# Cluster-masked attention and a SwiGLU layer as one pass over head pairs: mask inside the K=128 score product, the feed-forward work of batch b-1 between the chunks of batch b, and the cast of v behind the last use of its buffer

## Chip, cores and metric

The kernel runs on one core of one Trainium2 chip. The metric is the device time of one execution in microseconds (us). Engines are named as the profile names them: PE is TensorE (matmul), PEld its weight loads, DVE is VectorE, ACT is ScalarE, POOL is GpSimd, and SP is SyncE, which here only issues DMAs.

## What is computed

The shapes are B=4 batches, H=8 heads, S=768 tokens, D=64, 16 clusters per head, d_model=512 and d_ff=1536. All inputs and the output are float32.

```
c_n      = centroids / (||centroids|| + 1e-6)               # per head, 16 x 64
q_assign = argmax over clusters of (q/||q||) . c_n          # the same for k
mask     = q_assign[:, :, :, None] == k_assign[:, :, None, :]
scores   = where(mask, q k^T / sqrt(D), -1e9)
attn     = softmax(scores)
x        = (attn v), heads side by side: 3072 tokens x 512
xn       = x / rms(x) * rms_g
out      = (silu(xn w_gate) * (xn w_val)) w_out             # 3072 x 512
```

## The kernel before

There are two stages, one after the other. The first loops over the 32 (batch, head) pairs. For each it loads q, k and v as six blocks of 128 tokens, and casts v to bf16 with a column of ones behind it (L69), which later gives the row sums. It transposes q and k on PE, one float32 block of 128x64 at a time (L93, L97), and two engines copy each result out of PSUM (a bf16 copy by ACT, a float32 copy by DVE). The cluster scores are float32 matmuls of 16 output partitions (L108, `scT_ps`); ACT copies them to SBUF, POOL takes the maximum over the 16 partitions (L113, `sc_max`), and DVE compares (L114). The result is a one-hot matrix of 16 x 768 for q and for k.

The attention matrix is made transposed, keys on partitions, in 12 tiles of 128x384. Each has two matmuls, the scores with 64 rows in use (L121, `sc_ps`) and the mask as the product of the two one-hot matrices with 16 rows in use (L123, `mk_ps`). ACT takes the exponential (L126) and DVE multiplies it by the mask into `pT` (L127). Then, for each of six groups of queries, six matmuls of 65 columns (L132, `acc`) give the weighted sum of v and the row sum, DVE divides (L134 to L136), and a DMA writes 128x64 to a buffer `x_scratch` in DRAM.

The second stage first loads the three weight matrices (3 MB each), casts them to bf16 on DVE (L154 to L161), and then takes 512 tokens at a time: it reads x back, normalizes, transposes on PE (L186), does the gate and value products (L194, L196, 512 columns each), SiLU on ACT (L199), the product on DVE (L200), the output product (L205), a copy and a store. ACT loads another function table whenever it goes from exp or SiLU to the square root and back.

Nothing is written out by hand as an order. The pools have two buffers for most tiles, and a scheduler orders the instructions of each engine.

## Time and profile before

| | before |
|---|---|
| time, median of 3 runs | 1065.87 us (1063.18 to 1066.9) |
| span of the profiled execution | 1065.2 us |
| PE, DVE, ACT, POOL busy | 908.9, 598.0, 508.9, 167.2 us |
| mean granted TensorE clock | 0.718 |

Only the profiled execution's span is recorded, not a separate time; the median of the runs is 0.7 us above that span. A busy PE is not a PE at its peak: the recorded length of a matmul has a tail that overlaps the next one, so the pace is read from one start to the next. Granted clock 1.00 is the upper of TensorE's two levels (2.4 GHz), 0.50 the lower (1.2 GHz).

### The profile page before, as it was taken

How to read it: one execution, taken by the hardware profiler on the slowest of the kernel's cores; microseconds unless marked ns; L12 is line 12 of the kernel's file. 1: busy time of each engine (PE TensorE's matmuls, PEld its weight loads, DVE VectorE, ACT ScalarE, POOL GpSimd, SP SyncE). 2: the span in 40 equal slices, each digit the busy share in tenths (PEclk: the TensorE clock that was granted, in tenths of full speed). 3: DMA queues.
4: the chain of work that ended last, by engine and by line, in shares of the span. 5: the costliest groups of instructions: out<-in, count | busy, mean ns of one | idle time of the engine just before them, and what ended most of it. 6: DMA issues, size and time to landing. Idle time of an engine off the chain costs nothing.

```text
span 1065.2 us, 11986 instructions
## 1 busy us (share of the span) xinstructions
PE 908.9 (85%) x3552; PEld 311.0 (29%) x3552; DVE 598.0 (56%) x1665; ACT 508.9 (48%) x1221; POOL 167.2 (16%) x72
## 2 busy tenths in 40 slices
...
DMA packets 114098, 41.82 MB, mean 39 GB/s; under 512 B 105328, under 2 KB 108400, under 8 KB 114032
## 3 DMA queue, kind: packets, MB, share of 16 engines
...
## 4 chain that ended last, share of the span: by engine, by line
PE 57%; issue 23%; POOL 7%; DVE 4%; ACT 4%; DMA 4%; POOLq 0%; SPq 0%; DVEq 0%; ACTq 0%
PE scT_ps L108 11%; PE mk_ps L123 9%; PE sc_ps L121 8%; POOL sc_max L113 6%; PE gps L194 6%; PE ops L205 6%; PE vps L196 6%; PE ttmp L97 4%; PE ttmp L93 3%; PE acc L132 3%; DMA wo_tmp<-in_moe_w_out_dram 1%; ACT scT_sb L111 1%; PE tps L186 1%; ACT xnT L187 1%; DMA wtmp<-in_moe_w_val_dram 1%
## 5 line engine op out<-in xcount | busy, mean ns | idle before, releaser
L127 DVE TENSOR_TENSOR pT<-p_e,mk_ps 128x384 bf16<-128x384 bf16 x384 | 209.9, 553 | 157.1 <-PE mk_ps L123 140.3
L113 POOL PARTITION_ALL_REDUCE sc_max<-scT_sb x64 | 166.1, 2602 | 598.7 <-ACT scT_sb L111 597.5
L123 PE MATMUL mk_ps<-q_ohT,k_ohT 16*128 16x384 bf16 x384 | 184.8, 498 | 45.5 <-DVE o_sb L136 41.1
L121 PE MATMUL sc_ps<-qT,kT 64*128 64x384 bf16 x384 | 182.8, 492 | 23.5 <-ACT p_e L126 22.0
L126 ACT ACTIVATE p_e<-sc_ps 128x384 bf16<-128x384 f32 x384 | 168.3, 483 | 18.0 <-DVE pT L127 11.7
L98 ACT CAST kT<-ttmp 64x128 bf16<-64x128 f32 x192 | 49.6, 258 | 175.9 <-PE ttmp L97 174.4
L111 ACT COPY scT_sb<-scT_ps 16x384 f32<-16x384 f32 x128 | 59.6, 466 | 107.9 <-PE scT_ps L108 107.8
L194 PE MATMUL gps<-xnT,wg 128*128 128x512 bf16 x288 | 106.3, 396 | 0.8 <-ACT sg L199 0.2
L196 PE MATMUL vps<-xnT,wv 128*128 128x512 bf16 x288 | 105.9, 394 | 0.0
L132 PE MATMUL acc<-v_bf,pT 128*128 128x65 bf16 x1152 | 93.9, 244 | 7.2 <-DVE o_sb L136 6.6
L123 PEld LDWEIGHTS <-k_ohT 16*128 16x128 bf16 x384 | 37.6, 100 | 212.7 <-issue 138.7
L132 PEld LDWEIGHTS <-pT 128*128 128x128 bf16 x1152 | 77.0, 131 | 57.5 <-DVE qT L95 22.1
L108 PE MATMUL scT_ps<-qT,c_nT 64*16 64x384 f32 x128 | 93.0, 829 | 0.1
L94 ACT CAST qT<-ttmp 64x128 bf16<-64x128 f32 x192 | 49.4, 257 | 86.1 <-PE ttmp L93 85.9
L97 PE MATMUL ttmp<-ident_f,k_in 128*64 128x128 f32 x192 | 79.7, 415 | 9.7 <-DVE kT L99 5.5
L108 PE MATMUL scT_ps<-kT,c_nT 64*16 64x384 f32 x128 | 87.0, 794 | 0.0
L200 DVE TENSOR_TENSOR gvT<-sg,vps 128x512 bf16<-128x512 f32 x72 | 47.7, 685 | 67.8 <-ACT sg L199 67.1
L93 PE MATMUL ttmp<-ident_f,q_in 128*64 128x128 f32 x192 | 79.9, 416 | 1.0 <-DVE qT L95 1.0
L187 ACT COPY xnT<-tps 128x128 bf16<-128x128 bf16 x96 | 21.5, 266 | 105.0 <-DVE wo L161 51.4
L121 PEld LDWEIGHTS <-kT 64*128 64x128 bf16 x384 | 35.9, 101 | 108.1 <-issue 104.8
L186 PE MATMUL tps<-ident,xn 128*128 128x128 bf16 x96 | 19.6, 238 | 55.2 <-ACT xnT L187 53.7
L205 PE MATMUL ops<-wo,gvT 128*128 128x512 bf16 x288 | 66.7, 379 | 0.0
...
## 6 DMA issues: line engine op xcount, KB each, us to landing
...
x_scratch<-o_sb SPq DMA_DIRECT2D x192, 16.0 KB, 1.5
...
wtmp<-in_moe_w_gate_dram SPq DMA_DIRECT2D x1, 3072.0 KB, 10.0
...
```

The source lines that it names most:

```text
L93: nc.tensor.transpose(ttmp, q_in[:, t, :], ident_f32)
L97: nc.tensor.transpose(ttmp2, k_in[:, t, :], ident_f32)
L108: nc.tensor.matmul(scT_ps, lhsT=c_nT, rhs=src_T[:, m * MM:(m + 1) * MM], start=True, stop=True)
L113: nc.gpsimd.partition_all_reduce(sc_max, scT_sb, NC, bass_isa.ReduceOp.max)
L121: nc.tensor.matmul(sc_ps, lhsT=kT[:, kc, :], rhs=qT_flat[:, m * MM:(m + 1) * MM], start=True, stop=True)
L123: nc.tensor.matmul(mk_ps, lhsT=k_ohT[:, kc * P:(kc + 1) * P], rhs=q_ohT[:, m * MM:(m + 1) * MM], start=True, stop=True)
L126: nc.scalar.activation(p_e, sc_ps, ACT.Exp, scale=scale)
L127: nc.vector.tensor_mul(pT[:, kc, m * MM:(m + 1) * MM], p_e, mk_ps)
L132: nc.tensor.matmul(acc, lhsT=pT[:, kc, qg * P:(qg + 1) * P], rhs=v_bf[:, kc, :], start=(kc == 0), stop=(kc == ST - 1))
L194: nc.tensor.matmul(gps, lhsT=wg[:, dc, fc * P:(fc + 1) * P], rhs=xnT[:, dc, :], start=(dc == 0), stop=(dc == DC - 1))
L196: nc.tensor.matmul(vps, lhsT=wv[:, dc, fc * P:(fc + 1) * P], rhs=xnT[:, dc, :], start=(dc == 0), stop=(dc == DC - 1))
L205: nc.tensor.matmul(ops, lhsT=gvT[:, fc, s * P:(s + 1) * P], rhs=wo[:, fc, :], start=(fc == 0), stop=(fc == FC - 1))
```

## The change

The program becomes one pass over 32 slots, one per (batch, head), in an order that is written out by hand (`tc.manual_schedule()`). A slot has 9 chunks, each a score tile of 128x512, so there are 288 chunks.

- **Mask in the score matmul.** The tiles `aug` hold, on 128 partitions, 64 rows of transposed q or k in bf16, 16 one-hot rows and zeros. On q's side the one-hot rows are 0 for the token's cluster and -2048 elsewhere, so one matmul over K=128 adds -2048 to each score whose clusters differ, and the exponential makes it zero. `mk_ps` and the DVE multiply are gone.
- **Head pairs.** Two heads are transposed together, as 128x128 float32 blocks, in groups of four (`t_group`), with one copy of 512 columns per group. POOL casts into `aug` (`casts`) and into `vbf` (`casts_v`). The cluster scores are four float32 matmuls of 32 output columns that lie at partitions 0, 32, 64 and 96 of one PSUM tile (`assign`). DVE transposes them, takes the maximum along the free axis and compares, and eight DMAs put the one-hot rows into `aug` (`argmax1`, `argmax2`).
- **x stays on chip.** One division per slot writes into `x_t`; there is no `x_scratch`.
- **Feed-forward between the chunks.** Chunk 87 is the first that carries a piece of the layer for batch 0; from there each chunk of batch b carries one piece for batch b-1, which is four matmuls of 384 columns (gate or value) or three of 512 (output). There are 288 such pieces, and 12 empty ones at the beginning. What is left when the chunks end, all of batch 3, follows as a tail. SiLU becomes `tanh` and a DVE operation, so that all of ACT's functions but the first square root are in one table.
- **Weights** are loaded and cast in 12 parts during the first slots.
- **Place of the v cast.** For pair pi, `casts_v` stands at step 9 of the pair before, which is behind the last use of that `vbf` buffer (steps 2 to 7 of the same slot, for the second head of pair pi-2).

The core of the diff (`+` lines are in program order, and everything of the old body is removed):

```diff
+MASK = 2048.0
...
-    x_scratch = nc.dram_tensor("x_scratch", (n_tokens, d_model), BF16, kind="Internal").ap()
...
-                        sc_ps = ps.tile([P, MM], F32, tag="scores")
-                        mk_ps = ps.tile([P, MM], F32, tag="mask")
-                        nc.tensor.matmul(sc_ps, lhsT=kT[:, kc, :], rhs=qT_flat[:, m * MM:(m + 1) * MM],
-                                         start=True, stop=True)
-                        nc.tensor.matmul(mk_ps, lhsT=k_ohT[:, kc * P:(kc + 1) * P], rhs=q_ohT[:, m * MM:(m + 1) * MM],
-                                         start=True, stop=True)
-                        p_e = sb1.tile([P, MM], BF16, tag="p_e")
-                        nc.scalar.activation(p_e, sc_ps, ACT.Exp, scale=scale)
-                        nc.vector.tensor_mul(pT[:, kc, m * MM:(m + 1) * MM], p_e, mk_ps)
...
+    ps_sc = ctx.enter_context(tc.tile_pool(name="ps_sc", bufs=2, space=PSUM))
+    ps_gv = ctx.enter_context(tc.tile_pool(name="ps_gv", bufs=2, space=PSUM))
+    ps_d = ctx.enter_context(tc.tile_pool(name="ps_d", bufs=1, space=PSUM))
+    ps_pv = ctx.enter_context(tc.tile_pool(name="ps_pv", bufs=1, space=PSUM))
+    ps_t = ctx.enter_context(tc.tile_pool(name="ps_t", bufs=2, space=PSUM))
...
+    def load_pair(pi):
+        b, hp = divmod(pi, NP)
+        tiles = []
+        for src, nm in ((q, "q_in"), (k, "k_in")):
+            tl = ld.tile([P, ST, 2, D], F32, name=nm, tag=nm)
+            for a in range(2):
+                nc.sync.dma_start(out=tl[:, :, a, :],
+                                  in_=src[b, 2 * hp + a].rearrange("(p t) d -> p t d", p=P))
+            tiles.append(tl)
+        tl = ld.tile([P, 2, ST * D], F32, name="v_in", tag="v_in")
+        nc.sync.dma_start(
+            out=tl, in_=v[b, 2 * hp:2 * hp + 2].rearrange("h (p t) d -> p h (t d)", p=P))
+        tiles.append(tl)
+        loads[pi] = tiles
...
+            tl = const.tile([P, 2, S], BF16, name=f"aug{i}{a}")
+            nc.gpsimd.memset(tl, 0.0)
+            row.append(tl)
+        aug.append(row)
+        tl = const.tile([P, 2, ST, D + 1], BF16, name=f"vbf{i}")
+        nc.gpsimd.memset(tl, 1.0)
+        vbf.append(tl)
+    D0 = (0, D)
+    O0 = (D, 0)
...
+    def w_load(i):
+        kind, j = divmod(i, 4)
+        wt = stage.tile([P, DF], F32, name="wt", tag="wt", bufs=4)
+        if kind < 2:
+            src = (moe_w_gate, moe_w_val)[kind]
+            nc.sync.dma_start(out=wt, in_=src[j * P:(j + 1) * P, :])
...
+        def t_group(g):
+            if g == 0:
+                qk32[0] = prep.tile([P, 2 * S], F32, name="qk32", tag="qk32")
+            q_in, k_in, v_in = loads[pi]
+            tp = ps_t.tile([P, 4, P], F32, name="tp", tag="t")
+            for i in range(4):
+                side, t = divmod(4 * g + i, ST)
+                src = (q_in, k_in)[side]
+                nc.tensor.transpose(tp[:, i, :], src[:, t, :, :].rearrange("p a d -> p (a d)"), ident_f)
+            dst = qk32[0][:, g * 512:(g + 1) * 512]
+            if g == 1:
+                nc.vector.tensor_copy(dst, tp[:, :, :].rearrange("p a b -> p (a b)"))
+            else:
+                nc.scalar.copy(dst, tp[:, :, :].rearrange("p a b -> p (a b)"))
+        def casts():
+            for a in range(2):
+                r = slice(D0[a], D0[a] + D)
+                nc.gpsimd.tensor_copy(aug[st][a][r, :, :].rearrange("p s n -> p (s n)"), qk32[0][r, :])
+        def casts_v():
+            v_in = loads[pi][2]
+            for a in range(2):
+                nc.gpsimd.tensor_copy(vbf[st][:, a, :, 0:D],
+                                      v_in[:, a, :].rearrange("p (t d) -> p t d", d=D))
...
+        def assign():
+            hp = pi % NP
+            sp = ps_t.tile([P, HS], F32, name="sp", tag="t")
+            for j in range(4):
+                nc.tensor.matmul(sp[32 * j:32 * j + 32, :], lhsT=cbd[:, hp, :],
+                                 rhs=qk32[0][:, j * HS:(j + 1) * HS], start=True, stop=True,
+                                 tile_position=(0, 32 * j))
+            state["sp"] = sp
+        def argmax1():
+            tr = prep.tile([P, HS], F32, name="tr", tag="tr")
+            nc.vector.transpose(tr, state["sp"])
+            mx = small.tile([P, HS // NC], F32, name="mx", tag="mx")
+            trv = tr[:, :].rearrange("p (n c) -> p n c", c=NC)
+            nc.vector.tensor_reduce(mx, trv, axis=AX, op=ALU.max)
+            state["tr"], state["mx"] = trv, mx
+        def argmax2():
+            oh = prep.tile([P, HS], BF16, name="oh", tag="oh")
+            nc.vector.tensor_tensor(oh[:, :].rearrange("p (n c) -> p n c", c=NC), state["tr"],
+                                    state["mx"].unsqueeze(2).to_broadcast([P, HS // NC, NC]), op=ALU.is_ge)
+            nc.vector.tensor_scalar(oh[0:64, :], oh[0:64, :], scalar1=1.0, scalar2=MASK,
+                                    op0=ALU.subtract, op1=ALU.mult)
+            ohT = prep.tile([P, HS], BF16, name="ohT", tag="ohT")
+            nc.vector.transpose(ohT, oh)
+            for a in range(2):
+                for j in range(4):
+                    side, half = divmod(j, 2)
+                    nc.sync.dma_start(
+                        out=aug[st][a][O0[a]:O0[a] + NC, side, half * HS:(half + 1) * HS],
+                        in_=ohT[32 * j + NC * a:32 * j + NC * a + NC, :])
+        return [lambda: t_group(0), lambda: t_group(1), lambda: t_group(2), casts, assign, argmax1, argmax2, casts_v]
...
+    def score_chunk(slot, j):
+        pi, a = divmod(slot, 2)
+        ag = aug[pi % 2][a]
+        if j == 0:
+            pts[slot] = ptp.tile([P, ST * S], BF16, name="pT", tag="pT")
+        sc = ps_sc.tile([P, CH], F32, name="sc", tag="sc")
+        lo = j * CH
+        while lo < (j + 1) * CH:
+            kc, qo = divmod(lo, S)
+            n = min((j + 1) * CH - lo, S - qo)
+            o = lo - j * CH
+            nc.tensor.matmul(sc[:, o:o + n], lhsT=ag[:, 1, kc * P:(kc + 1) * P],
+                             rhs=ag[:, 0, qo:qo + n], start=True, stop=True)
+            lo += n
+        nc.scalar.activation(pts[slot][:, j * CH:(j + 1) * CH], sc, ACT.Exp, scale=scale)
...
+    def pv_group(slot, g):
+        pi, a = divmod(slot, 2)
+        vb = vbf[pi % 2]
+        if g == 0:
+            accs[slot] = ps_pv.tile([P, ST, D + 1], F32, name="acc", tag="acc")
+        acc = accs[slot]
+        for kc in range(ST):
+            nc.tensor.matmul(acc[:, g, :], lhsT=pts[slot][:, kc * S + g * P:kc * S + (g + 1) * P],
+                             rhs=vb[:, a, kc, :], start=(kc == 0), stop=(kc == ST - 1))
+    def pv_norm(slot):
+        b, h = divmod(slot, H)
+        if h == 0:
+            x_t[b] = xp.tile([P, ST, DM], BF16, name="x", tag="x")
+        acc = accs.pop(slot)
+        inv = small.tile([P, ST, 1], F32, name="inv", tag="inv")
+        nc.vector.reciprocal(inv, acc[:, :, D:D + 1])
+        nc.vector.tensor_tensor(x_t[b][:, :, h * D:(h + 1) * D], acc[:, :, 0:D],
+                                inv.to_broadcast([P, ST, D]), op=ALU.mult)
...
+        def sumsq(t):
+            if t == 0:
+                st["ss"] = small.tile([P, ST], F32, name="ss", tag="ss")
+                st["jk"] = xp.tile([P, 2, DM], BF16, name="jk", tag="jk")
+            if t % 2 == 0:
+                nc.scalar.activation(st["jk"][:, 0, :], x_t[b][:, t, :], ACT.Square,
+                                     accum_out=st["ss"][:, t:t + 1])
+            else:
+                nc.vector.scalar_tensor_tensor(st["jk"][:, 1, :], x_t[b][:, t, :], 1.0, x_t[b][:, t, :],
+                                               op0=ALU.mult, op1=ALU.mult, accum_out=st["ss"][:, t:t + 1])
+        def inv():
+            ir = small.tile([P, ST], F32, name="ir", tag="ir")
+            nc.gpsimd.tensor_scalar(ir, st["ss"], scalar1=1.0 / DM, scalar2=eps, op0=ALU.mult, op1=ALU.add)
+            nc.gpsimd.tensor_tensor(ir, ir, mhalf, op=ALU.pow)
+            st["ir"] = ir
...
+    def ffn_piece(n, kind, tail):
+        half = n // FC
...
+            if kind == 0 and fc == 0:
+                gvT[half] = ffn.tile([P, FC, HS], BF16, name="gvT", tag="gvT")
+            w = (wg, wv)[kind]
+            pool, tag = (ps_sc, "sc") if tail and n % 2 else (ps_gv, "gv")
+            pt = pool.tile([P, CH], F32, name=("gp", "vp")[kind], tag=tag)
+            for dc in range(DC):
+                nc.tensor.matmul(pt[:, :HS], lhsT=w[:, dc, fc * P:(fc + 1) * P],
+                                 rhs=xnT[b][:, dc, m * HS:(m + 1) * HS],
+                                 start=(dc == 0), stop=(dc == DC - 1))
+            if kind == 0:
+                th = ffn.tile([P, HS], F32, name="th", tag="th")
+                nc.scalar.activation(th, pt[:, :HS], ACT.Tanh, scale=0.5)
+                uu = ffn.tile([P, HS], F32, name="uu", tag="uu")
+                def after():
+                    nc.vector.scalar_tensor_tensor(uu, th, 1.0, pt[:, :HS], op0=ALU.add, op1=ALU.mult)
+                cur[n] = uu
+            else:
+                uu = cur.pop(n)
+                def after():
+                    nc.vector.tensor_tensor(gvT[half][:, fc, :], uu, pt[:, :HS], op=ALU.mult)
+            pend.append(after)
+        elif kind == 2 and half >= 1:
+            hf = half - 1
+            b, m = divmod(hf, 2)
+            t = m * TH + fc // 4
+            qd = fc % 4
+            if qd == 0:
+                pool, tag = (ps_pv, "acc") if tail and (fc // 4) % 2 else (ps_d, "d")
+                cur["d"] = pool.tile([P, DM], F32, name="dp", tag=tag)
+            dp = cur["d"]
+            for i in range(3):
+                f = qd * 3 + i
+                tl = fc // 4
+                nc.tensor.matmul(dp, lhsT=gvT[hf][:, f, tl * P:(tl + 1) * P], rhs=wo[:, f, :],
...
+    def at(slot, step, fn):
+        slot += step // NCH
+        extra.setdefault((slot, step % NCH), []).append(fn)
+    for pi in range(1, B * NP):
+        s0 = 2 * (pi - 1)
+        parts = prep_parts(pi)
+        for fn, step in zip(parts, (1, 3, 5, 6, 8, 9, 10, 9)):
+            at(s0, step, fn)
+        if pi + 1 < B * NP:
+            at(s0, 8, lambda pi=pi: load_pair(pi + 1))
+    for i in range(4):
+        at(0, i, lambda i=i: w_load(i))
+    for i in range(12):
+        at(2, 3 * i, lambda i=i: w_cast(i))
+        if i + 4 < 12:
+            at(2, 3 * i + 1, lambda i=i: w_load(i + 4))
+    for b in range(B):
+        steps = (8, 8, 9, 9, 10, 10, 11, 11, 12, 12, 13, 13)
+        for fn, step in zip(rms_parts(b), steps):
+            at(H * (b + 1), step, fn)
+    FFN0 = 15
+    for slot in range(NS):
+        for j in range(NCH):
+            score_chunk(slot, j)
+            done = slot * NCH + j
+            limit = min(B, max(0, (done - FFN0) // (H * NCH))) * 2 * FC
+            ffn_next(limit)
+            flush(1)
+            if slot > 0 and 2 <= j < 2 + ST:
+                pv_group(slot - 1, j - 2)
+            if slot > 0 and j == 2 + ST:
+                pv_norm(slot - 1)
+            for fn in extra.get((slot, j), ()):
+                fn()
...
+    for j in range(2 * NCH):
+        slot = NS
+        ffn_next(2 * FC * (B - 1) + (FC if False else 0), tail=False)
+        flush(1)
+        if 0 <= j < ST:
+            pv_group(NS - 1, j)
+        if j == ST:
+            pv_norm(NS - 1)
+        for fn in extra.get((NS + j // NCH, j % NCH), ()):
+            fn()
+    while ffn_next(NU + FC, tail=True):
+        flush(1)
+    flush()
```

The order on PE changes throughout. Before, inside a head of the first stage, this is what stands there; `sc_ps` and `mk_ps` alternate, and the transposes of the next head (`ttmp`) stand between:

```order
L121 MATMUL sc_ps<-qT,kT 128x384
L123 LDWEIGHTS k_ohT
L123 MATMUL mk_ps<-q_ohT,k_ohT 128x384
L97 MATMUL ttmp_383<-ident_f_63,k_in 64x128
L121 LDWEIGHTS kT
L121 MATMUL sc_ps<-qT,kT 128x384
```

After, in a chunk of a slot past chunk 87, one group of four transposes of the next pair ends the chunk before, then come one score matmul of 512 columns and the first matmuls of a gate piece; six `acc` matmuls follow behind the fourth `gp`:

```order
L184 MATMUL tp<-ident_f,k_in 128x128 x4
L253 LDWEIGHTS aug_127
L253 MATMUL sc<-aug_127 128x512
L339 LDWEIGHTS wg
L339 MATMUL gp<-xnT,wg 128x384
```

The mask matmul has left, and feed-forward matmuls stand behind every score tile. On SP, which issues every DMA, this is the beginning of the first stage before:

```order
L64 DMA q_in<-in_q_dram 128x6x64
L65 DMA k_in<-in_k_dram 128x6x64
L66 DMA v_in<-in_v_dram 128x6x64
L72 DMA c_in<-in_centroids_dram 16x64
```

And this is SP after, from the first weight loads to the one-hot rows of the third pair:

```order
L152 DMA wt<-in_moe_w_gate_dram 128x1536 x4
L76 DMA q_in<-in_q_dram 128x6x64 x2
L76 DMA k_in<-in_k_dram 128x6x64 x2
L80 DMA v_in<-in_v_dram 128x2x384
L232 DMA aug_133<-ohT 16x384 x4
L232 DMA aug_135<-ohT 16x384 x4
L152 DMA wt<-in_moe_w_val_dram 128x1536 x3
```

The eight DMAs that a pair's scores need stand behind the five loads of the pair after next, and in the first slots behind weight loads too.

## Rows read from the trace of the kernel before

**Rows 1.** The page's first part: busy time, share of span, instructions by engine.

```profile
PE 908.9 (85%) x3552; PEld 311.0 (29%) x3552; DVE 598.0 (56%) x1665; ACT 508.9 (48%) x1221; POOL 167.2 (16%) x72
```

**Rows 2.** Busy time by stretch: length, engines, granted clock (PEclk), DMA share, GB/s.

```profile
0.00:25.50 25.50, 11.60 (x26) 2.96 (x26) 10.16 (x41) 9.29 (x27) 6.11 (x10) 1.00 0.38 78
25.50:790.00 764.50, 680.73 (x2566) 213.00 (x2566) 474.34 (x1418) 380.69 (x965) 161.10 (x62) 0.65 0.13 28
790.00:836.50 46.50, 0.37 (x2) 0.24 (x3) 11.22 (x10) 0.28 (x2) 0.00 (x0) 0.50 0.55 204
836.50:1065.20 228.70, 216.22 (x958) 94.77 (x957) 102.27 (x198) 118.66 (x228) 0.00 (x0) 0.95 0.11 40
```

**Rows 3.** Groups of instructions by line: busy us, mean ns, idle before, releaser.

```profile
L113 POOL PARTITION_ALL_REDUCE sc_max<-scT_sb x64 | 166.1, 2602 | 598.7 <-ACT scT_sb L111 597.5 <-DVE q_ohT L114 1.1
L123 PE MATMUL mk_ps<-q_ohT,k_ohT 16*128 16x384 bf16 x384 | 184.8, 498 | 45.5 <-DVE o_sb L136 41.1 <-DVE k_ohT L114 3.5 <-DVE pT L127 0.9
L200 DVE TENSOR_TENSOR gvT<-sg,vps 128x512 bf16<-128x512 f32 x72 | 47.7, 685 | 67.8 <-ACT sg L199 67.1 <-PE vps L196 0.7
```

**Rows 4.** PE's instructions in order, first stage: start us, length us, what, count.

```profile
524.45 1.46 PE L108 MATMUL scT_ps<-qT,c_nT 64*16 64x384 f32 x2
525.84 0.49 PE L123 MATMUL mk_ps<-q_ohT,k_ohT 16*128 16x384 bf16 x1
526.26 0.42 PE L93 MATMUL ttmp<-ident_f,q_in 128*64 128x128 f32 x1
526.48 0.54 PE L132 MATMUL acc<-v_bf,pT 128*128 128x65 bf16 x6
526.82 0.41 PE L97 MATMUL ttmp<-ident_f,k_in 128*64 128x128 f32 x1
...
529.89 0.81 PE L108 MATMUL scT_ps<-kT,c_nT 64*16 64x384 f32 x2
530.63 0.20 PE L83 MATMUL cnt_ps<-ident_f,c_n 16*64 16x16 f32 x1
...
531.09 0.30 PE L97 MATMUL ttmp<-ident_f,k_in 128*64 128x128 f32 x1
531.32 0.82 PE L108 MATMUL scT_ps<-kT,c_nT 64*16 64x384 f32 x2
532.44 0.56 PE L132 MATMUL acc<-v_bf,pT 128*128 128x65 bf16 x12 [0.30 <-DVE o_sb L136]
532.93 0.49 PE L121 MATMUL sc_ps<-qT,kT 64*128 64x384 bf16 x2
```

**Rows 5.** Busy time in two short stretches, columns as in group 2.

```profile
529.00:535.00 6.00, 4.64 (x25) 1.42 (x23) 4.10 (x9) 5.22 (x11) 4.32 (x2) 0.93 0.37 78
...
876.00:880.00 4.00, 3.13 (x15) 1.48 (x14) 1.91 (x4) 2.62 (x12) 0.00 (x0) 0.75 0.40 131
```

**Rows 6.** PE's instructions in order, beginning of the second stage.

```profile
842.87 0.63 PE L196 MATMUL vps<-xnT,wv 128*128 128x512 bf16 x1
843.29 0.63 PE L194 MATMUL gps<-xnT,wg 128*128 128x512 bf16 x1
...
844.01 0.38 PE L194 MATMUL gps<-xnT,wg 128*128 128x512 bf16 x1
...
845.52 0.38 PE L196 MATMUL vps<-xnT,wv 128*128 128x512 bf16 x1
```

**Rows 7.** ACT's instructions in order: two exponentials, and two SiLU, back to back.

```profile
102.58 0.86 ACT L126 ACTIVATE p_e<-sc_ps 128x384 bf16<-128x384 f32 x2
...
849.14 1.08 ACT L199 ACTIVATE sg<-gps 128x512 f32<-128x512 f32 x2
```

**Rows 8.** POOL's memset of the identity, by line.

```profile
masks.py:197 POOL MEMSET ident_f<- 128x128 f32 x1 | 0.2, 204 | 0.0
```

**Rows 9.** DMA issues: KB each, median us from issue to landing.

```profile
x_scratch<-o_sb SPq DMA_DIRECT2D x192, 16.0 KB, 1.5
```

**Rows 10.** The last instruction on DVE, in order of time.

```profile
1061.63 0.69 DVE L207 COPY out_sb<-ops 128x512 f32<-128x512 f32 x1 [1.90 <-PE ops L205]
```

290 lines of the change are left out of this document (142 added, 148 removed).

## Prediction

> **What bounds the kernel now.** I read the busy time by stretch first, since the shares of the whole span mix stages. It shows three stages and a start [rows 2]: 25.5 us until the first full tile, 764.5 us of attention with PE busy 89% of it (680.7), 46.5 us in which PE does almost nothing while the weights arrive and are cast, and 228.7 us of feed-forward with PE busy 95%. So PE ends last in both long stages; DVE, the next, is busy 62% of the attention stretch (474.3 of 764.5), and 56% of the whole span [rows 1].
>
> Why attention takes PE so long is seen in its instructions in order [rows 4]. The reader should look at starts, not lengths. From the mask matmul at 525.84 to the transpose at 526.26 is 0.42 us. Its 384 columns need less: in the second stage a matmul of 512 columns takes the same 0.42 us from start to start as long as the clock is at its lower level (842.87 to 843.29), and 0.216 us afterwards (844.01 to 845.52 are seven intervals) [rows 6]. So 384 columns are worth 0.32 us at the lower level, and 0.10 us is the weight load, which lies bare where matmuls of 64 and 16 rows alternate. The second cause is the clock. The mean length of all 384 mask matmuls is 498 ns [rows 3], which is what single ones have at granted 0.50 (0.49 at 525.84), so nearly the whole stage runs at the lower level. It can rise: from about 529.9 on the same stage runs at the upper one, after a run of transposes, `acc` and float32 matmuls with no bare loads between [rows 4, 5]. A float32 matmul of 384 columns (two records) then takes 0.74 us from start to start (529.89 to 530.63) where it took 1.39 (524.45 to 525.84).
>
> **The change, in prices of these rows.** Taken away are 384 mask matmuls with about 0.42 us of pace each, their bare loads, the 46.5 us without PE work (the weights come in the first slots), `x_scratch` and its waits, and 64 all-reduces of 2602 ns on POOL [rows 3]. No PE work of the feed-forward is saved: 288 pieces of 1536 columns are the same columns as before. It cannot hide under attention either, if PE is the bound of both; what the interleaving does is fill PE. So I sum PE, and then ask whether another engine exceeds it.
>
> Prices at the upper level, and the lower in brackets:
> - bf16 columns with K=128: 512 in 0.216 (0.427) us [rows 6]. A slot's 4608 score columns cost 1.94 (3.84) us; a piece, 0.65 (1.28).
> - `acc`, 65 columns: twelve in 0.49 us (532.44 to 532.93), 0.041 each; six in 0.34 us at the lower level, 0.057 [rows 4]. 36 per slot: 1.48 (2.05) us.
> - float32 transpose: 0.23 (531.09 to 531.32) and 0.22 at the lower level when an `acc` follows (526.26 to 526.48) [rows 4]. No row has a stationary block of 128 float32 columns; here it was 64. From below, the clock could halve 0.22 to 0.11; from above, the load could double with its columns, which adds the 0.12 us by which 0.23 exceeds that, so 0.35. I take 0.23, the row nearest. 12 per pair, 6 per slot: 1.38 us (0.7 to 2.1; lower level 1.3).
> - `assign`: four float32 matmuls of 384 columns per pair. One after the other, 4 x 0.74 = 2.96 us (5.56) per pair, 1.48 (2.78) per slot [rows 4]. From below: all four at once, 0.37 per slot. I take one after the other, as every pair of such matmuls in the trace goes.
> - the transposes of x, 96 of 128 bf16 columns in all: under 0.3 us per slot by columns and a fixed part.
>
> A slot without feed-forward costs PE 1.94 + 1.48 + 1.38 + 1.48 = 6.3 us (10.0 at the lower level). A slot with nine pieces costs 9 x 0.65 + 6.3 + 0.3 = 12.4 us (22.0).
>
> The other engines, per slot. **ACT**: two SiLU of 512 columns back to back take 1.08 us, two exponentials of 384 take 0.86 [rows 7], so 0.54 and 0.43 each at most. Nine exponentials and one copy are 5.4 us, three tanh 1.3, squares and x copies about 0.4: 5.4 without and 7.1 us with feed-forward. **DVE**: no operation that it gets is wider than 512 columns but the weight casts and two copies of 768 per batch, and the 512-wide product out of PSUM takes 685 ns [rows 3]. Six feed-forward operations, two for the division, half of five for the one-hot rows, and about two for copies and norms: 12.5 x 0.685 = 8.6 us at most. **POOL** casts 2 x 1536 and 2 x 384 columns per pair, which no row shows. The memset, 128 columns in 204 ns [rows 8], gives 1.6 ns per column and 6.1 us per pair; the all-reduce, 768 in 2602 ns [rows 3], gives 3.4 and 13.0 us. I take the lower half, the memset being the simple streaming operation, but either fits under a pair's 12.6 us without feed-forward (nearly) and 24.8 with. So PE stays the bound of every slot, at either level of the clock, and the DVE and ACT work is covered by it. Should PE come out faster than these rows, DVE at up to 8.6 us would be next.
>
> **The sum.** Start: the chain to the first scores is the same kind as before (loads, transposes, cluster scores, maximum, one-hot rows), with DMAs in place of the all-reduce: 25 us, as now [rows 2]. Chunks 0 to 86 are 9.67 slots without feed-forward: 61 us at the upper level, 97 at the lower. I take 7.0 us per slot, 68, one fifth of the way: everything here has K=128, as in the stretch after which the clock rose [rows 4, 5], and no waits are due, but the first pairs share SP and the DMA engines with 9 MB of weights. Chunks 87 to 287 are 22.33 slots, 277 us less 12 empty pieces (7.8): 269. Then the last head: 15 pieces (9.8), `acc` 1.5, and a stand of about 3 us while the last x is normalized, since DVE and ACT must pass over it before PE can transpose. The tail is 72 + 12 = 84 pieces, 54.6 us. After the last matmul come a copy and a store, 3.6 us as now (1061.63 to the end of the span at 1065.2) [rows 10]. That is 72.5. Together 25 + 68 + 269 + 72.5 = 434.5, say 435 us against a span of 1065.2; the median of the runs lies 0.7 us above that span, which changes nothing here.
>
> **Where v's cast stands.** `casts_v` at step 9 comes after the last `acc` that reads its buffer (steps 2 to 7), so POOL does not stop there with the next pair's `casts` behind it. Its next reader is `acc` at step 2 of the second slot after, 11 or more chunks later, 8 us at 0.7 us per chunk: covered. Any earlier place would have made POOL wait up to that step, which the same margin covers at 1.4 us per chunk; I cost this part at nothing.
>
> **A rule against the serial price.** In the rows the cluster-score matmuls follow one another at 0.74 us, but they all write partitions 0 to 15 [rows 4]. The Trainium skill ("TensorE: Matmul & The Clock Gate", Part 3) says that matmuls whose outputs lie in different 32-partition strips run at the same time. No run here shows that so far. By it `assign` would be one matmul's time, not four.
>
> **Rivals.**
> - *The four cluster matmuls run together.* As a mechanism of this kernel: the pair pays 0.74 us, not 2.96; 1.1 us per slot over 32 slots is 35 us, and the time is 400. For it speaks that the four share the moving data's layout and write four strips; against it only that no row has it. With transposes at their low end as well, 378.
> - *The next pair is late.* The first scores of a pair need POOL's two casts and four of the eight DMAs, which stand on SP behind five loads, and land 1.5 us after issue if like `x_scratch` [rows 9]. The steps from 8 or 10 to 18 leave 5.6 to 7 us at 0.7 us per chunk, 11 or more with feed-forward. If PE stands 3 us at each of 15 pairs, the clock falls as well: with PE busy 3.13 of 4 us in the second stage the mean was 0.75 [rows 5], and 4 us at the lower level lose 2. That is 15 x 5 = 75 us, 510. For it: the chain crosses four engines. Against: the margin with feed-forward is double.
> - *The clock stays low.* If the small `acc` matmuls and the transposes keep it down as they mostly did: 25 + 97 + (22.33 x 22.0 - 12 x 1.28 = 476) + (15 + 84) x 1.28 + 2 + 5 + 3.6 = 735 us. Against: dense matmuls of K=128 had raised it by 844.0, 7.5 us into the second stage [rows 2, 6], and more than half of every slot's PE time is such.
> - *Slower than before: POOL's casts.* They gate every pair. The change loses from the point at which a pair takes 633 us / 15 = 42 us longer than 25, that is 67 us of POOL work, 17 ns per column. The dearest row has 3.4. Then 1068 us or more.
>
> **How the numbers follow.** The forecast, PE-bound at the upper level with cluster matmuls in sequence, 435 us, has 0.45; cluster matmuls together 0.28; pairs late 0.18; clock low 0.08; slower 0.01. The range from 378 (the second case with transposes at their low end) to 540 (pairs late, with transposes at their high end, 22 us, and a little more) leaves out the low clock and thin ends, about 0.15. A difference of 0.3% is about what a measurement of this kernel can tell from none; all cases but one are far beyond it: faster 0.98, same 0.01, slower 0.01.
>
> **What would show it.** In the changed profile PE should be busy nearly all of each slot from chunk 87 on, at granted clock near 1.00, with 11 to 12.5 us per slot, and 6 to 7 before; ACT and DVE well under PE; two table loads only; DMA landings and POOL's casts never on the chain of waits past the start. Whether the four `assign` matmuls start together or 0.74 us apart decides between the first two cases. The forecast is wrong if the granted clock is below 0.8 in the middle, if PE's idle time at a pair's first `sc` is put down to `aug`, or if ACT takes more per chunk than PE.

## The result, and the profile after

The changed kernel takes 419.35 us (median of 4 runs, 417.93 to 422.39) against 1064.53 us before, a ratio of 0.3946 with a 95% interval of 0.3929 to 0.3962. The forecast was 435 us, the range 378 to 540. The profiled execution has a span of 417.7 us and a mean granted clock of 0.939. Ratios, here and below, leave out any execution that is more than 1.5% above the fastest of its kernel.

The page's first part, and the beginning of its fourth (the chain that ended last), as answers to [rows 1]:

```profile
PE 355.3 (85%) x2972; PEld 219.9 (53%) x3009; DVE 224.8 (54%) x446; ACT 242.4 (58%) x460; POOL 80.5 (19%) x87
...
PE 75%; DVE 9%; SPq 4%; DMA 4%; ACT 3%; POOL 2%; issue 2%; POOLq 0%; DVEq 0%; ACTq 0%
```

PE is still what ends last, busy for the same 85% of a span that is 0.39 of the old one. This is the busy time by stretch of the changed kernel, cut at the first score matmul (20.2), the first gate piece (108.5), the end of the last chunk (341) and the first piece of the tail (358); columns as in [rows 2]:

```profile
0.00:20.20 20.20, 4.60 (x21) 2.76 (x22) 10.25 (x17) 3.94 (x5) 11.90 (x19) 0.89 0.55 120
20.20:108.50 88.30, 58.28 (x552) 38.33 (x554) 40.35 (x72) 54.55 (x104) 24.55 (x22) 0.81 0.62 183
108.50:341.00 232.50, 222.94 (x1994) 140.68 (x2021) 135.38 (x281) 161.33 (x306) 42.51 (x44) 0.98 0.25 65
341.00:358.00 17.00, 14.76 (x114) 8.94 (x115) 11.44 (x29) 5.72 (x14) 1.52 (x2) 0.90 0.05 16
358.00:417.70 59.70, 54.68 (x295) 29.24 (x299) 27.38 (x50) 16.84 (x34) 0.00 (x0) 1.00 0.12 45
```

The long stretch is as forecast: PE busy 96% of it, granted clock 0.98. The 88 us before it are not: PE is busy only 66%, the clock is at 0.81 in the mean, and the DMA engines are busy 62%. Against the terms of the sum:

| stretch | forecast, us | measured, us |
|---|---|---|
| start | 25 | 20.2 |
| chunks 0 to 86 | 68 | 88.3 |
| chunks 87 to 287 | 269 | 232.5 |
| last head and last x | 14.3 | 17.0 |
| tail with the last store | 58.2 | 59.7 |
| together | 434.5 | 417.7 |

Two large errors of opposite sign stand in this table, one of 20 and one of 36 us. PE's instructions in order, in the middle of the long stretch, show the second:

```profile
200.65 0.35 PE L267 MATMUL acc<-vbf,pT 128*128 128x65 bf16 x6
200.84 0.63 PE L184 MATMUL tp<-ident_f,k_in 128*128 128x128 f32 x4
201.31 0.38 PE L253 MATMUL sc<-aug 128*128 128x512 bf16 x1
201.53 0.81 PE L339 MATMUL gp<-xnT,wg 128*128 128x384 bf16 x4
202.18 0.35 PE L267 MATMUL acc<-vbf,pT 128*128 128x65 bf16 x6
...
204.38 0.85 PE L208 MATMUL sp<-qk,cbd 128*32 128x384 f32 x8
205.17 0.39 PE L253 MATMUL sc<-aug 128*128 128x512 bf16 x1
```

From start to start, a score tile of 512 columns takes 0.22 us and a gate piece 0.65, as priced. Six `acc` matmuls take 0.19 us (0.032 each, priced 0.041), four float32 transposes 0.47 (0.12 each, priced 0.23), and the four cluster matmuls 0.79 us together (204.38 to 205.17, eight records, priced 2.96). A slot is then 1.94 + 1.15 + 0.70 + 0.40 = 4.2 us without and 10.4 us with feed-forward, and 22.33 x 10.4 less 7.8 is 224 us. PE's idle time in the stretch is about the rest, 9.6 us (232.5 - 222.9); two thirds of it come when the transposes of x wait for DVE's norm (6.5 us in two places).

The first error is seen in who waited for whom, PE alone over the whole span (us in total, times, longest):

```profile
PE sc L253 <- DMA aug<-ohT: 26.1, 5, 6.9
PE xtp L313 <- DVE xn L306: 12.5, 4, 4.3
PE c_ps L135 <- DVE c L133: 8.7, 1, 8.7
PE sc L253 <- ACT pT L256: 4.7, 11, 0.5
PE acc L267 <- POOL vbf L199: 1.6, 1, 1.6
```

and in PE's order of time, where the scores of pairs 1, 2, 3 and 4 begin:

```profile
38.68 1.01 PE L253 MATMUL sc<-aug 128*128 128x512 bf16 x3 [6.29 <-DMA aug<-ohT]
...
57.12 1.01 PE L253 MATMUL sc<-aug 128*128 128x512 bf16 x3 [5.80 <-DMA aug<-ohT]
...
76.31 1.01 PE L253 MATMUL sc<-aug 128*128 128x512 bf16 x3 [5.61 <-DMA aug<-ohT]
...
90.40 0.59 PE L253 MATMUL sc<-aug 128*128 128x512 bf16 x3 [1.48 <-DMA aug<-ohT]
```

This is the rival of the late pair, but only in the pairs ahead of the feed-forward: 19.2 us of waits (the fifth, 6.9 us, belongs to the start), and behind the three long ones PE runs at the lower clock for a while (three score records take 1.01 us at 76.31 and 0.59 at 90.40). In the same stretch the first transposes of x wait 4.3 us for the norm, and one `acc` group 1.6 us for POOL's cast of v. Past chunk 87 there is no wait for one-hot rows. And since PE needs 4.2 us per slot ahead of the feed-forward and ACT, by the prediction's prices, 5.4, ACT and not PE would set the pace there if nothing were late: 9.67 x 5.4 = 52 us.

### The profile page after: what moved, and what is told of

Its sections match the earlier page's. It is cut to its first block, busy times and chain, and to the rows that moved or that the text cites. A ratio compares the mean times of both kernels' runs of the same rounds, so it can differ in the third digit from the quotient of the medians.

```text
span 417.7 us, 7771 instructions
## 1 busy us (share of the span) xinstructions
PE 355.3 (85%) x2972; PEld 219.9 (53%) x3009; DVE 224.8 (54%) x446; ACT 242.4 (58%) x460; POOL 80.5 (19%) x87
## 3 DMA queue, kind: packets, MB, share of 16 engines
HBM read 28.35 MB, written 6.29 MB: 83 GB/s over the span
## 4 chain that ended last, share of the span: by engine, by line
PE 75%; DVE 9%; SPq 4%; DMA 4%; ACT 3%; POOL 2%; issue 2%; POOLq 0%; DVEq 0%; ACTq 0%
PE vp L339 15%; PE sc L253 14%; PE gp L339 14%; PE dp L368 14%; PE acc L267 7%; PE tp L184 6%; DMA aug<-ohT 3%; PE xtp L313 3%; PE sp L208 2%; SPq L76 2%; DVE jk L294 2%; SPq L232 1%; ACT pT L256 1%; DVE oh L223 1%; DVE c L133 1%
## 5 line engine op out<-in xcount | busy, mean ns | idle before, releaser
L256 ACT ACTIVATE pT<-sc 128x512 bf16<-128x512 f32 x288 | 166.9, 598 | 77.8 <-PE sc L253 75.2
L253 PE MATMUL sc<-aug 128*128 128x256 bf16 (+1 forms) x381 | 111.4, 342 | 30.9 <-DMA aug<-ohT 26.1
L348 DVE SCALAR_TENSOR_TENSOR uu<-th,gp 128x384 f32<-128x384 f32 x96 | 53.0, 552 | 78.0 <-ACT th L344 78.0
L194 POOL CAST aug<-qk 64x1536 bf16<-64x1536 f32 x32 | 47.5, 1486 | 224.6 <-ACT qk L189 173.2
L339 PE MATMUL vp<-xnT,wv 128*128 128x384 bf16 x384 | 80.1, 332 | 1.7 <-DVE gvT L354 1.6
L339 PE MATMUL gp<-xnT,wg 128*128 128x384 bf16 x384 | 78.0, 326 | 0.0
L368 PE MATMUL dp<-wo,gvT 128*128 128x512 bf16 x254 | 69.1, 379 | 2.9 <-ACT ob L374 1.1
L267 PE MATMUL acc<-vbf,pT 128*128 128x65 bf16 x1152 | 69.6, 196 | 1.9 <-POOL vbf L199 1.6
L344 ACT ACTIVATE th<-gp 128x384 f32<-128x384 f32 x96 | 47.3, 492 | 40.9 <-PE gp L339 38.4
L354 DVE TENSOR_TENSOR gvT<-uu,vp 128x384 bf16<-128x384 f32 x96 | 52.6, 548 | 7.9 <-PE vp L339 1.3
```

The costliest lines, as they stand in the source:

```text
L194: nc.gpsimd.tensor_copy(aug[st][a][r, :, :].rearrange("p s n -> p (s n)"), qk32[0][r, :])
L253: nc.tensor.matmul(sc[:, o:o + n], lhsT=ag[:, 1, kc * P:(kc + 1) * P], rhs=ag[:, 0, qo:qo + n], start=True, stop=True)
L256: nc.scalar.activation(pts[slot][:, j * CH:(j + 1) * CH], sc, ACT.Exp, scale=scale)
L267: nc.tensor.matmul(acc[:, g, :], lhsT=pts[slot][:, kc * S + g * P:kc * S + (g + 1) * P], rhs=vb[:, a, kc, :], start=(kc == 0), stop=(kc == ...
L339: nc.tensor.matmul(pt[:, :HS], lhsT=w[:, dc, fc * P:(fc + 1) * P], rhs=xnT[b][:, dc, m * HS:(m + 1) * HS], start=(dc == 0), stop=(dc == DC ...
L344: nc.scalar.activation(th, pt[:, :HS], ACT.Tanh, scale=0.5)
```

## The experiments

**More cluster matmuls in one strip.**

```diff
-            for j in range(4):
+            for j in (0, 0, 0, 0, 1, 2, 3):
                 nc.tensor.matmul(sp[32 * j:32 * j + 32, :], lhsT=cbd[:, hp, :],
```

> The changed kernel with three more cluster matmuls per pair, all into the same 32 partitions as the first one (their result is overwritten with the same values). Theory: matmuls into one strip follow one another at 0.74 us, and only those into different strips share their time (the four of the changed kernel take 0.79 us together). Then 16 pairs x 3 x 0.74 = 36 us more, less what falls into waits in the first five pairs: 445 to 456 us. Rival: the short time of the four has nothing to do with strips (fewer passes for a block of 32 columns, say): then three more cost three times a quarter of 0.79, 0.6 us per pair, 10 us in all, 427 to 430.

Measured: 441.92 us (440.16 to 443.88), ratio 0.4145 (0.4128 to 0.4163), 22.6 us more than the changed kernel. PE's order in this run:

```profile
218.47 2.77 PE L208 MATMUL sp<-qk,cbd 128*32 128x384 f32 x14
221.16 0.39 PE L253 MATMUL sc<-aug 128*128 128x512 bf16 x1
```

Seven matmuls take 2.69 us, four times 0.67, where four in different strips took 0.79. So matmuls into one strip go one after the other, and those into other strips share their time. The profile is 24.4 us longer than the changed kernel's (442.1 against 417.7). Of these, 17.2 lie behind the first gate piece, where ten pairs with 1.90 us more each should give 19.0, and 7.2 ahead of it (it starts at 115.7, and not at 108.5), where six pairs give less because they wait anyway (their waits for one-hot rows fall from 26.1 to 23.2 us). The expectation had 0.74 us for each added matmul, and 0.63 (1.90 / 3) is what it cost; over 16 pairs that is 5 us, which covers the 3 us by which its window was missed.

**Feed-forward not interleaved.**

```diff
-            xnT[b] = xp.tile([P, DC, S], BF16, name="xnT", tag="xnT")
+            xnT[b] = xp.tile([P, DC, S], BF16, name="xnT", tag="xnT", bufs=4)
...
-            limit = min(B, max(0, (done - FFN0) // (H * NCH))) * 2 * FC
-            ffn_next(limit)
+            ffn_next(0)
...
-        ffn_next(2 * FC * (B - 1) + (FC if False else 0), tail=False)
+        ffn_next(0, tail=False)
```

> The feed-forward is not interleaved: all 288 pieces come after the last head (four buffers for the transposed x in place of two). Theory: interleaving hides the attention's ACT time and the pairs' hand-off under feed-forward matmuls. Chunks 87 to 287 then cost ACT's 5.4 us per slot or a little more instead of PE's 4.2, 22.33 x 5.4 to 6.5 = 121 to 145 us, and the pieces 187 us, where they took 232 + 55 us together: 440 to 465 us. Rival: PE is the bound of both parts, so that the order of its work does not matter: 22.33 x 4.2 + 187 is what it takes now, 415 to 425.

Measured: 463.52 us for the profiled execution (span 461.7), the fastest of four (463.52 to 477.97, median 472.95); a single one gives no ratio. The busy time from chunk 87 to the end of the last chunk, and what PE waited for in it:

```profile
103.96:255.50 151.54, 117.98 (x1326) 77.17 (x1322) 61.72 (x135) 123.99 (x239) 46.41 (x44) 0.95 0.31 77
```

```profile
PE sc L253 <- DMA aug<-ohT: 12.1, 8, 1.6
PE sc L253 <- ACT pT L256: 11.6, 29, 0.6
PE xtp L313 <- DVE xn L306: 8.5, 2, 4.2
```

A slot of attention alone takes 6.8 us (151.5 / 22.33), ACT busy 5.6 of it and PE 5.3 as the profile counts it, so neither is busy throughout (82% and 78%). The 151.5 us lie above the 121 to 145 that were expected for this part; the whole, 463.52, came out near the upper end of its window. One-hot rows are late in eight places past chunk 87, where the changed kernel has none, although the weights have long been loaded. So the theory stands in its direction: interleaving is worth 44 us in these profiles (461.7 - 417.7), and 48 from chunk 87 on (357.7 against 309.4), because the feed-forward covers ACT's time and the pair's hand-off; the stand at the norm of x it covers in part. The prediction's words "it cannot hide under attention either, if PE is the bound of both" are right as a condition, but PE is not the bound of an attention slot.

**v's cast earlier.**

```diff
-        for fn, step in zip(parts, (1, 3, 5, 6, 8, 9, 10, 9)):
+        for fn, step in zip(parts, (1, 3, 5, 6, 8, 9, 10, 2)):
```

> casts_v of the next pair stands at step 2 instead of step 9, ahead of casts at step 6 on POOL, so POOL stops there until the last acc of the pair before the last has read the buffer (step 7). Theory: POOL has time to spare (80 us busy of 418) and the wait is covered where a pair lasts 20 us, so 0 past chunk 87; in the first four pairs casts come about one step late, but the scores wait for the one-hot rows and not for the casts: 0 to 3 us more, 418 to 422. Rival: the wait holds up casts, and with them the next pair's scores, at every pair: 15 x 1.5 = 22 us more, 440.

Measured: 421.91 us (420.52 to 423.0), ratio 0.3965 (0.3953 to 0.3977), whose interval overlaps that of the changed kernel. The expectation was wrong about what the place does. The buffer's readers and writers are kept in the order of the program, so with the cast at step 2 the `acc` groups at steps 3 to 7 read the next pair's v, and for the second head of each pair this kernel computes something else. The trace agrees: POOL waits only for the group at step 2 (waits for `acc` of 81.6 us in 19 places), and the groups behind it wait for the new cast (0.9 us in four places). The time is the same within the intervals. That does not mean that nothing moved: the first scores of pair 2 wait 6.6 us with POOL's cast of v as the last thing, where they waited 5.8 us for one-hot rows.

**Who is late in the first pairs: the order on SP, or the weights.**

```diff
-            at(s0, 8, lambda pi=pi: load_pair(pi + 1))
+            at(s0, 0, lambda pi=pi: load_pair(pi + 1))
```

> The loads of the pair after next stand at step 0 of a pair instead of step 8, so ahead of nothing that is due soon. The PE waits for the one-hot rows in the first pairs (6.3, 5.8, 5.6, 1.5 us) are blamed on one of two things. Theory A: the order on SP; the eight small DMAs stand behind five loads. Then the waits shrink to below 2 us each and the clock stays up between: 400 to 406 us. Theory B: the 9 MB of weights, which fill the DMA engines and hold up whatever SP issues behind them. Then moving the pair loads alone changes little: 414 to 420.

```diff
-    for i in range(4):
-        at(0, i, lambda i=i: w_load(i))
-    for i in range(12):
-        at(2, 3 * i, lambda i=i: w_cast(i))
-        if i + 4 < 12:
-            at(2, 3 * i + 1, lambda i=i: w_load(i + 4))
+    for i in range(12):
+        at(0, 3 + 6 * i, lambda i=i: w_load(i))
+        at(0, 15 + 6 * i, lambda i=i: w_cast(i))
```

> The twelve weight loads stand 6 chunks apart (steps 3, 9, 15, ... from slot 0) and each cast 12 chunks behind its load; pair loads stay at step 8. Theory A (order on SP): the waits of the first pairs stay at about the 1.5 us of the fourth pair, or more, 410 to 418. Theory B (weights): they fall to between 0 and 1.5 us, with the low clock that follows them: 398 to 406.

Both edits together:

> Pair loads at step 0 and weight loads spread. If the two causes add, it is below either alone; if one of them is the whole cause, it equals that one within 2 us. Without any wait for one-hot rows the first 87 chunks would be set by ACT at 5.4 us per slot, 52 us, where they now take 88: the least that is to be had is about 385, and 395 to 402 is expected, since the division, the casts and the start of the feed-forward still make PE stand.

Measured: pair loads first 421.14 us, ratio 0.3955 (0.3946 to 0.3964); weights spread 417.06, 0.3918 (0.3903 to 0.3934); both 417.42, 0.3918 (0.3899 to 0.3938). The first is no change. The second and third are about 2 us less, at the edge of what the intervals separate from the changed kernel (0.3929 to 0.3962), and equal each other; the 395 to 402 us that were expected of both together did not come. PE's wait for one-hot rows in the three runs, in this order, with 6.2 to 6.9 us of the start in each:

```profile
PE sc L253 <- DMA aug<-ohT: 25.5, 5, 7.4
```

```profile
PE sc L253 <- DMA aug<-ohT: 21.7, 5, 6.9
```

```profile
PE sc L253 <- DMA aug<-ohT: 19.5, 5, 6.2
```

So neither is the whole cause, but both were on the path. In the changed kernel the one-hot rows of pair 1 are ready on DVE at 30.74, and SP begins to issue their DMAs at 33.88, because it is still issuing loads of the pair after next behind four weight loads:

```profile
26.23 6.81 SPq L76 DMA_DIRECT2D k_in<-in_k_dram  x2
...
33.88 5.54 SPq L232 DMA_DIRECT2D aug<-ohT  x8
```

That is 3.1 of the 6.29 us for pair 1, and 0.7 and 0.6 us for the next two. With the pair loads first SP issues these DMAs as soon as the rows are ready (30.38), but the landing that PE waits for now takes 7.71 us where it took 2.90:

```profile
30.38 0.58 SPq L232
...
31.63 7.71 DMA aug<-ohT
```

The wait moved from the issue to the landing. The chain of waits of the run with both edits shows what is left between the cluster matmuls of a pair and its first score:

```profile
26.74 0.83 PE sp L208 x8
27.59 0.59 DVE tr L215
...
29.87 0.59 DVE ohT L228
30.48 0.58 SPq L232
31.10 0.60 SPq L232
31.74 2.95 DMA aug<-ohT
34.78 1.01 PE sc L253 x3
```

That is 8.0 us, from step 8 to the next pair, which is ten chunks of 0.54 to 0.6 us: too long by 2.0 to 2.6 us, and PE waits 2.7. Two weight loads had been issued 4 us ahead of these DMAs, so a part of the 2.95 us of landing may be theirs (the median landing is 1.8).

**Preparation earlier.** With the pair loads at step 0 as well:

```diff
-        for fn, step in zip(parts, (1, 3, 5, 6, 8, 9, 10, 9)):
+        for fn, step in zip(parts, (0, 1, 2, 3, 4, 4, 5, 9)):
```

> The next pair's preparation stands earlier: transposes at steps 0, 1, 2, casts at 3, cluster matmuls and first half of the maximum at 4, comparison and the eight DMAs at 5 (they were 1, 3, 5, 6, 8, 9, 10), with the pair loads at step 0; v's cast stays at 9, weights as in the changed kernel. Neither order on SP nor the weights explained the waits of the first pairs. Theory C: a chunk without feed-forward lasts 0.54 us (ACT), and the chain from the cluster matmuls through five DVE operations and four DMA issues of 0.6 us to the landing is 8 to 9 us, longer than the ten chunks from step 8 to the next pair. With four steps and more of head start (fourteen chunks, 7.6 us) the waits fall from 19 us in four pairs to below 6, and the clock does not drop there: 398 to 406. Rival: what is late is a DMA landing behind weight data, whenever it is issued: 412 to 420.

Measured: 422.56 us (419.15 to 425.93), ratio 0.3957 (0.3938 to 0.3975): no gain, and a little above the rival's window too. In its chain of waits:

```profile
27.64 8.45 DMA aug<-ohT
36.17 0.59 PE sc L253
```

The one-hot rows now leave at 27.6, 4 us earlier than in the run with both edits, and land at 36.1, behind the 3 MB of weights that were issued just ahead of them. Such a DMA takes 1.8 us (median of all 128). For this pair the longer lead is eaten up by the landing. Two other things in this profile go against each other: its first score starts at 17.18 us and not at 20.20, which is told with the next run, and past chunk 87 PE waits 10.7 us in ten places for the feed-forward product of DVE (`gvT`), where the changed kernel has 1.3 us in three. All runs with the preparation at these steps have that wait.

**Late memsets.** The `aug` and `vbf` tiles of the second set are filled behind `prep_parts(0)`:

```diff
+            if i == 0:
+                nc.gpsimd.memset(tl, 0.0)
...
+        if i == 0:
+            nc.gpsimd.memset(tl, 1.0)
...
     for part in prep_parts(0):
         part()
+    for a in range(2):
+        nc.gpsimd.memset(aug[1][a], 0.0)
+    nc.gpsimd.memset(vbf[1], 1.0)
```

> The memsets of the second set of aug and vbf (3.4 us of POOL) stand behind the first pair's casts. In the start, DVE's scaling of the 16 centroids of 8 heads took 4.34 us for two operations of 64 columns and ended when POOL's memsets did. Theory: DVE cannot run that operation while POOL's memset holds what the two share, so the start is 3.4 us shorter: 414 to 416. Rival: that length is something else (a first use, a load), and the start stays: 417 to 420.

Measured: 416.7 us (414.46 to 419.1), ratio 0.3919 (0.3903 to 0.3935), 2.6 us less, with an interval that just touches the changed kernel's. In the changed kernel's start (its timeline) the two DVE operations of 64 columns end when POOL's last memset does:

```profile
4.21 4.34 DVE L133 TENSOR_SCALAR c<-c_in,c_t 128x64 f32<-128x64 f32 x2
...
5.08 2.70 POOL L108 MEMSET aug<- 128x1536 bf16 x2
...
7.71 0.75 POOL L112 MEMSET vbf<- 128x780 bf16 x1
```

In this run, whose memsets end at 5.1 us, the same two take 0.93:

```profile
4.29 0.93 DVE L135 TENSOR_SCALAR c<-c_in,c_t 128x64 f32<-128x64 f32 x2
```

and the first score starts at 17.15 us instead of 20.20. But the edit is not the only way there. In the run with early preparation the memsets stand where they stood, and the same operations took 1.05 us, between two memsets:

```profile
4.18 1.05 DVE L133 TENSOR_SCALAR c<-c_in,c_t 128x64 f32<-128x64 f32 x2
...
5.09 2.78 POOL L108 MEMSET aug<- 128x1536 bf16 x2
```

The run without interleaving has the same (0.89 us, first score at 17.26). So of eight profiles with the memsets in place, DVE came through between two of them in two and waited for the last of them in six, and what decides that is not shown. The late memsets take the chance away; that they are the cause of the 2.6 us is not shown by the times. The Trainium skill ("GPSIMD Engine Reference", 1. Specifications) says that POOL's way to SBUF is shared with VectorE, with contention where a VectorE instruction runs in a two-port mode or has two inputs in SBUF. That DVE ends 0.1 us behind a memset in each of these profiles agrees with a shared way; which mode the operation ran in is not shown, and `c_sq`, with both inputs in SBUF, took 0.23 us beside the first memset.

**All of it.** Early preparation, pair loads at step 0, spread weights, late memsets:

> All that helped or should: preparation early, pair loads at step 0, weight loads spread, late memsets. Theory C adds the 2.6 us of the memsets and about 2 of the spread weights to the run with early preparation: 392 to 402. If the waits of the first pairs are set by the DMA engines alone: 410 to 415, the sum of the spread weights and the late memsets.

Measured: 411.41 us (410.39 to 412.75), ratio 0.387 (0.386 to 0.388): faster than the kernel before and the changed one, at the bottom of the rival's window and above the theory's. The other parts' sum would be 419.35 - 2.3 - 2.6 = 414.4. What each run gained and lost, by one profile of each (the columns follow one another in time, in us):

| run | first score, us | to the first gate piece | to the last chunk's score | to the end |
|---|---|---|---|---|
| changed kernel | 20.2 | 88.3 | 231.5 | 77.6 |
| both edits | 20.2 | 83.1 | 231.9 | 77.8 |
| late memsets | 17.2 | 88.1 | 231.2 | 77.7 |
| early preparation | 17.2 | 89.3 | 236.4 | 78.2 |
| all | 17.1 | 79.7 | 234.0 | 78.2 |

Early preparation gains nothing in the first 87 chunks by itself, and 3.4 us more than both edits when the weights are spread as well; past chunk 87 it costs 2 to 5 us. The stretches of this run up to the first gate piece at 96.8, and the long one:

```profile
17.10:97.00 79.90, 58.85 (x555) 38.38 (x556) 40.52 (x72) 55.08 (x105) 24.25 (x22) 0.82 0.75 213
97.00:330.00 233.00, 219.13 (x2007) 138.18 (x2006) 133.53 (x277) 159.09 (x304) 42.53 (x44) 1.00 0.23 62
```

The first still takes 8.3 us per slot, not 5.4, with the DMA engines busy 75% of it. PE waits 7.6 us for the division, which stands on DVE behind weight casts whose data has not landed, and 11.0 us for one-hot rows (6.2 of these in the start). Two more runs went after these, each with one edit on this kernel.

**Weights in another queue.** The loads in `w_load` are issued by ACT:

```diff
-            nc.sync.dma_start(out=wt, in_=src[j * P:(j + 1) * P, :])
+            nc.scalar.dma_start(out=wt, in_=src[j * P:(j + 1) * P, :])
...
-            nc.sync.dma_start(
+            nc.scalar.dma_start(
```

> The run with all changes, and the twelve weight loads issued by ACT, so in another DMA queue than the one-hot rows. With early preparation on top of unspread weights, the one-hot rows of the second pair took 8.5 us from issue to landing behind 3 MB of weights, and 3.1 us with spread weights; alone they take 1.8. Theory D1: they stand behind the weight data in the one queue of SP. Then landings fall to about 2 us, the waits for them (11 us in four, 6 of these in the start) to the start's 6 and at most 1 more, and the time to 403 to 408. Theory D2: the 16 DMA engines are shared, whatever queue issues: landings and time stay, 409 to 413.

Measured: 409.05 us (408.76 to 412.59), ratio 0.3844 (0.3833 to 0.3855), at the edge of the second theory's window, with an interval just below that of the run with all changes. The profiled execution is the longest of the five (412.59). Its waits of PE:

```profile
PE sc L255 <- ACT pT L258: 9.7, 13, 2.7
PE sc L255 <- DMA aug<-ohT: 6.9, 1, 6.9
...
PE sc L255 <- DMA q_in<-in_q_dram: 2.9, 2, 2.1
```

Only the start's wait for one-hot rows is left, as the first theory said; but its time did not come, since loads of q and k are late instead (one takes 7.1 us in the chain of waits, a one-hot row 4.8) and ACT, which now issues, is waited for longer (9.7 us, 5.3 before). So the queue set which transfer was late. That one still was fits DMA engines that all queues share, but no run separates that from the other waits.

**Casts later.**

```diff
-        at(0, 15 + 6 * i, lambda i=i: w_cast(i))
+        at(0, 21 + 6 * i, lambda i=i: w_cast(i))
```

> The run with all changes, and each weight cast 18 chunks behind its load instead of 12. There the weight casts stood in DVE's queue before their data had landed, with the division and the next pair's maximum behind them (PE waited 7.6 us for the division in three places). Theory: with six more chunks the data is there, those waits go, and 4 to 7 us with them: 404 to 408. Rival: PE's waits in the first 87 chunks only move to the next late thing (ACT's 5.4 us per slot, one-hot rows): 409 to 412.

Measured: 412.7 us (411.82 to 414.29), ratio 0.3876 (0.386 to 0.3893), no difference from the run with all changes. The waits for the division fall from 7.6 to 2.1 us, and those for one-hot rows grow from 11.0 to 17.3. So the wait moved, as the rival said, whose window ends 0.7 us below this time.

**The mask alone, on the kernel before.** One-hot rows go by DMA under the transposed q and k in tiles of 128 partitions:

```diff
+                    aT = qT if ohT is q_ohT else kT
+                    nc.sync.dma_start(out=aT[D:D + NC, :, :].rearrange("d t p -> d (t p)"), in_=ohT)
...
-                        nc.tensor.matmul(mk_ps, lhsT=k_ohT[:, kc * P:(kc + 1) * P], rhs=q_ohT[:, m * MM:(m + 1) * MM],
-                                         start=True, stop=True)
-                        p_e = sb1.tile([P, MM], BF16, tag="p_e")
-                        nc.scalar.activation(p_e, sc_ps, ACT.Exp, scale=scale)
-                        nc.vector.tensor_mul(pT[:, kc, m * MM:(m + 1) * MM], p_e, mk_ps)
+                        nc.scalar.activation(pT[:, kc, m * MM:(m + 1) * MM], sc_ps, ACT.Exp, scale=scale)
```

> The kernel before with one part of the change alone: the one-hot rows are written by DMA under the rows of transposed q and k in tiles of 128 partitions, one matmul over K=128 gives scores and mask, and the exponential writes pT; no mask matmul, no DVE multiply. All else is as before. Theory (bare weight loads and the extra matmul made PE's time): per head 12 x 0.32 + 12 x 0.33 + 4 x 1.39 + 2.05 = 15.4 us at the lower clock where it was 23.4, so the first stage is 490 us and the time 790; with the clock up, ACT's 12 us per head would bind, 680. Rival: the first stage hangs on the chain of each head through POOL's all-reduce, and little is won: above 950.

Measured: 955.57 us (953.23 to 957.55), ratio 0.898 (0.8958 to 0.9003). The rival is right. The first stage after this edit, and three of the waits (over the whole span):

```profile
25.00:690.00 665.00, 437.50 (x2184) 174.49 (x2185) 289.25 (x1065) 377.63 (x964) 158.56 (x63) 0.66 0.17 37
```

```profile
POOL sc_max L119 <- ACT scT_sb L117: 296.2, 30, 20.9
POOL sc_max L119 <- DVE inv L140: 177.0, 15, 12.5
DVE inv L140 <- PE acc L138: 165.9, 86, 9.1
```

PE falls from 89% to 66% busy, and the stage only from 764.5 to 665 us. Now no engine is busy more than 66% of it, so it hangs on the order of waits within and between heads: POOL's all-reduce waits for ACT's copy of the cluster scores and for the division, and the division for `acc`. Which link matters most is not shown. The granted clock from 240 to 690 us is 0.65 where it was 0.52: higher, but far from 1.00. (The 0.65 of [rows 2] for the whole old stage, and with it the mean of 0.718, is too high, since the profile reads 1.00 up to 238 us; there the cluster scores at 206.50 take 1.39 us from start to start, as they do at 524.45 [rows 4].) So the mask in the score matmul is worth 10% by itself. The rest of the gain lies in the other parts together (the order by head pairs, the maximum on DVE, x and weights on chip, the feed-forward between), of which only the interleaving has a run of its own.

## Why the prediction came out right

The time fell into the range and near the forecast, on the right mechanism for the long stretch, and by two errors that partly cancel: 36 us too dear there, 20 too cheap ahead of it. That the sum came within 4% is luck; that PE bounds the kernel from chunk 87 on is not. Two of the prediction's own signs of being wrong did appear ahead of chunk 87: PE's idle time at a pair's first `sc` is put down to `aug`, and ACT takes more per chunk than PE.

- **What bounds the kernel.** Right where it matters: from chunk 87 PE is busy 96% at granted clock 0.98, and the chain that ended last is 75% PE. The feed-forward pieces, score columns, tail and last store came out nearly as priced (59.7 against 58.2 us for the tail).
- **`assign` one after the other.** Wrong, and the rival with 0.28 was the case: 0.79 us per pair and not 2.96. The rule of the Trainium skill on 32-partition strips ("TensorE: Matmul & The Clock Gate", Part 3) agrees with the trace and with the run that added matmuls to one strip, in which one takes 0.67 us. This is 24 of the 36 us by which the long stretch was priced too dear (22.33 x 1.08).
- **Transposes and `acc`.** Mis-sized: 0.12 and 0.032 us where 0.23 and 0.041 were taken. The transposes came out at the lower bound of their range, not at the nearest row; the row had a 64-column block and other work around it. Together these are 1.0 us per slot, 22 us of the long stretch. Against them stand PE's 9.6 us of waiting there, which were not in the sum.
- **"No waits are due" in the first 87 chunks.** This step failed. The prediction named SP, the DMA engines and the 9 MB of weights as shared there, but put no wait into the sum, only a fifth of the way to the lower clock. The rival of the late pair had 3 us for each of 15 pairs; it was 5.6 to 6.3 us for three, 1.5 for one and none for the rest. Of its reasons, the order on SP behind the pair's loads was on the path (3.1 us of pair 1's wait), but moving the loads only moved the wait to the landing. POOL's casts into `aug` (2.98 us for two) held up no score there. What the runs show in place of "no waits" is a chain of 8 us against ten chunks that are shorter than forecast (0.54 to 0.6 us, and not 0.7), and DMA engines busy 62 to 75% of that stretch with 9 MB of weights, where the 12 KB transfer that PE waits for takes 2.9 to 3.9 us in the three long waits, and up to 8.45 us in the other runs.
- **PE as the bound of every slot.** Wrong for a slot without feed-forward. The prices there were PE 6.3 and ACT 5.4; with PE at 4.2 ACT is above it, and without interleaving PE waits for ACT's exponentials in 29 places past chunk 87 (11.6 us). The 6.8 us per slot of that run are more than ACT's time, so the hand-off and the norm of x bind there too.
- **The start.** 20.2 for 25 us, of which about 3 are DVE's wait for POOL's memsets, which some executions do not have. The prediction took the old start as a whole and looked into none of its parts.
- **The last x.** 17.0 for 14.3 us. The stand before PE's transposes is 1.7 us and not 3, but the clock falls there, and what follows runs at the lower level until about 357.
- **v's cast.** Nearly free, as said: one `acc` group waited 1.6 us for it, at 67.53. But the reason given for an earlier place (POOL would wait) was wrong: the program's order decides which v is read.
- **Low clock throughout, and slower than before.** Neither came. The clock falls where PE stands and comes back in the dense work behind each stand, eight times in the span (0.50 from 104 to 108 us, for example, behind the stand at the first norm, and 0.99 from 108 to 110). The prediction's remark that everything here has K=128, "as in the stretch after which the clock rose", misreads its rows: cluster scores on 64 rows stand there too.

What stays open is the exact share of chain and DMA traffic in the first 87 chunks. Every edit there moved at least a part of the wait to another place, and no run took the weights out of that stretch.
